# Softmax attention and a Mish layer, gated together, on one core: some normalising products on GpSimd, a new order, and another ending

## The chip, the cores and the metric

One core of a Trainium2 chip runs the kernel. The metric is device time in microseconds (us). The engines are TensorE (PE; PEld for its weight loads), VectorE (DVE), ScalarE (ACT), GpSimd (POOL) and SyncE (SP), which issues nearly all the DMAs.

## The reference

Two branches over 2048 tokens of width 640 are mixed by a gate per token.

```python
x = A_x                                             # 1 x 2048 x 640, bf16
g = sigmoid((x * gate_w).sum(-1, keepdims=True))
# A: 32 heads of 20
q, k, v = split_heads(x @ wqkv)
p = softmax(einsum("bhqd,bhkd->bhqk", q, k) * 20 ** -0.5)
a = merge_heads(einsum("bhqk,bhkd->bhqd", p, v)) @ wo
# B: 640 -> 1536 -> 640
h = einsum("bsd,df->bsf", x, w1) + b1
b = einsum("bsf,fd->bsd", h * tanh(softplus(h)), w2)
return g * a + (1 - g) * b
```

Both branches read the one x; an input B_x is taken and not used.

## The kernel before, in words

Queries are cut into 4 chunks of 512, heads into 8 groups of 4; a (chunk, group) pair is a group of work, and the last pair is cut into two of 256 queries. Each has 16 key tiles times 4 heads = 64 units, tiles of 128 keys x 512 queries. Three units make a step: 683 steps in all. For each step PE writes three score tiles into three PSUM banks (L1204), and ACT takes the exponential of all three in one instruction of 1536 columns (L1226, a wide step), or of two, 1024 columns (a narrow step). In a narrow step DVE evicts the third tile as an integer (L1271), and makes the exponential of it in pieces for up to four tiles at a time: fraction (L1335), product (L1339), power (L1343), all from SBUF to SBUF. Two sets of three banks alternate, so the scores of a step wait until ACT and DVE have read the step two before. PE multiplies the exponentials by V (L1463); a column of ones beside V sums them.

When a group ends, DVE copies the sums from PSUM to OUNG (L1552). SP turns the row of sums for the reciprocal (L1570), DVE inverts it (L1574), SP sends it to DRAM and back as a broadcast into BCT (L1575, L1581), and DVE multiplies OUNG by BCT (L1513): the normalising product, 128x512 in fp32 to bf16, into OTN for chunks 0 and 1 and into the free part of QT for chunks 2 and 3.

All else is fitted into gaps: projections, B's two matrix products, the Mish pieces on DVE, the output projection (L1048) and its mixture with B by the gate (L1054).

No loop of the chip's runs over this. The Python code is a planner: it lays out one straight list for each engine, by costs written in the file, and `pl.now` holds the time that it reckons each engine to be at. `work(until)` fills DVE's gaps from queues (`norm` for the normalising steps, `soon` for the pieces of the exponentials, `blend` for Mish, `bg`), `choose(s)` says whether step s is narrow, by DVE's lag and what is queued, and a table `NUDGE` shifts that choice for every eight steps. `Plan.run` gives the list out.

The last chunk's output projection is made in two parts: six groups early, into PART (fp32, in W2R's place), and the last two groups at the end. For the tokens of the second cut four tasks remain after the last exponential: two token tiles of 128 by two halves of 320 columns. One of them goes through ACT and POOL (L1902, L1904), three through DVE (L1054). Each half is stored by itself; SP issues six of these stores, ACT two (both L1080). Then each engine compares a flag and branches past a second program (for inputs whose exponents are too large), and SP waits for the stores:

```python
fast.run(eng, handle)
with handle.If(flags[eng] != 0):
    fast.wait_all(handle)
    full.run(eng, handle)
    ...
if eng == "sp":
    for op in outs:
        handle.wait_ge(fast.sems[op.key], op.count)
```

The line numbers that the prediction names are those of the kernel before. In the program after, the same steps have others: L1226 is L1287, L1271 is L1332, L1513 is L1576, L1054 is L1102, L1080 is L1131, L1993 is L2065.

Of the kernel before, what the change touches and what calls it, by code (L numbers as in the profile page):

```python
# [17 lines left out]
P = 128  # L18
# [5 lines left out]
NG = 8  # L24
# [13 lines left out]
OLD = 3  # L38
# [21 lines left out]
QUICK = 0.335  # L60
FAST = 0.335
# [8 lines left out]
RISK = {"pe": 0.1, "act": 0.3, "dve": 0.5, "pool": 1.2, "sp": 0.6}  # L70
CHAIN = 2.6
FILL = 2.5
GIVE_BACK = 40
# [9 lines left out]
SLOW_LOAD = 5.0  # L83
# [15 lines left out]
SPARE = 7  # L99
# [36 lines left out]
LEAD = 5  # L136
NUDGE = [0, 0, 0, 0, 0, 0, 0, 0, 0, 0, 0, 0, 0, 0, 0, 0, 0, 0, 0, 0, 0, 0, 0, 0, 0, 0, 0, 0, 0, 0, 0, 0, 0, 0, 0, 0, 0, 0, 0, 0, 0, 0, 0, 0, 0, 0, 0, 0, 0, 0, 0, 0, 0, 0, 0, -1, 0, 2, 0, 0, 0, 0, 0, 0, 0, 0.5, 3, 0, 0, 0, 3, 0, 1, 0.5, 0, 0, 0, 0, 0.5, 1, -0.5, 0, 0, -0.5, 0, 1]
# [12 lines left out]
class Plan:  # L150
# [3 lines left out]
    def __init__(self, prefix):  # L154
        self.prefix = prefix
        self.ops = []
        self.now = {e: 0.0 for e in ENGINES}
        self.kind = None
        self.passes = deque()
        self.queue = 0.0  # L160

    def add(self, eng, fn, deps=(), slot=None, cost=0.1, kind="F", tail=None, bulk=0.0):
        op = Op(eng, fn, [d for d in deps if d is not None], slot)
        at = self.now[eng]
        if eng == "pe":
            if kind != self.kind:
                at += SWITCH
                self.kind = kind
        for d in op.deps:
            if d.eng != eng or d.slot:  # L170
                at = max(at, d.t1 + HOP)
            elif eng == "dve":
                at = max(at, d.t1)
        self.now[eng] = at + cost
        if eng == "pe":
            self.passes.append((at + cost, cost))
        op.t1 = at + cost + (tail or (TAIL["sp"] if slot else TAIL[eng]))
# [42 lines left out]
    def run(self, eng, handle):  # L220
        for op in self.ops:
            if op.eng != eng:
                continue
# [25 lines left out]
def bass_gated_mix__softmax_full_mha__dense_activation_mish__prompt_kernel(  # L249
# [142 lines left out]
    def attention(pl, fast):  # L392
# [57 lines left out]
        def dve(fn, deps=(), cost=0.1, kind="F"):  # L450

            ready = max([pl.now["dve"], *(d.t1 + HOP for d in deps if d is not None)])
            work(ready + (LATER if fast and now["rate"] < BUSY and now["bank"] else SLACK))
            return pl.add("dve", fn, deps, cost=cost, kind=kind)
# [5 lines left out]
        def work(until):  # L460
            while True:
                best = None
                lined = sorted([lane for lane in (*soon, blend) if lane], key=lambda lane: lane[0][3])
                for rank, todo in enumerate((norm, *lined, bg)):
                    if todo:
                        cost, fn, dep = todo[0][:3]
                        op = dep() if dep else None
                        if op is False:
                            continue
                        begin = pl.now["dve"]  # L470
                        if op:
                            begin = max(begin, op.t1 if op.eng == "dve" and not op.slot else safe(op))
                        halve = len(todo[0]) > 4 and begin + cost > until
# [53 lines left out]
        if fast:  # L527
# [63 lines left out]
            q_blank = [pl.add("pool", lambda e, g=g: e.memset(QT[:, g, :], 0.0), cost=1.1) for g in range(1, NG)]  # L591
# [50 lines left out]
            def fetch(k, g, c, names):  # L642
# [14 lines left out]
                for dst, src in pairs:  # L657
                    op = pl.add("sp", lambda e, dst=dst, src=src: e.dma_start(dst, src), deps, slot, cost=0.5, bulk=1.3 if k else 0.1)
# [319 lines left out]
            def mish(ev, hb, hc, k):  # L978
# [9 lines left out]
                def piece(cost, fn, after=None):  # L988
                    def run():
                        last[0] = pl.add("dve", fn, [last[0]], cost=cost)  # L990
                        if after:
                            after(last[0])
                    blend.append((cost, run, lambda: last[0], due))
# [17 lines left out]
                piece(QUICK, scalar(B, W, MISH_IN))  # L1011
                piece(WIDE, times(B, W, B))
                piece(QUICK, scalar(B, B, MISH_MID))
                piece(WIDE, times(B, B, B))
                piece(QUICK, scalar(B, B, MISH_BY, MISH_BY * MISH_OUT))
# [55 lines left out]
        part_done = {}  # L1071

# [5 lines left out]
        def give(t, half, ev):  # L1078
            tb = (NC - 1) * 4 + t
            outs.append(pl.add(("sp", "act")[half and t in last_t], lambda e: e.dma_start(  # L1080
                out_ap[tb * P:(tb + 1) * P, of(half)], ended(t, half)), [ev], f"end{t}{half}", cost=0.6))

        def p_task(c, t, half, due, rest=False):
# [13 lines left out]
            def finish(bank, last):  # L1097
# [4 lines left out]
                add = PART[:, t, half, :] if rest else ball(tb)[:, of(half)]  # L1102
                if rest:
# [176 lines left out]
        def dve_by(fn, deps, cost, slack):  # L1280
# [3 lines left out]
            return pl.add("dve", fn, deps, cost=cost)  # L1284

        def close(batch):
# [15 lines left out]
            def piece(cost, fns, deps, after=None, split=False):  # L1302

                def run(some, each, mark):
                    def go():
                        for sp in some:
                            op = pl.add("dve", fns(sp), deps(), cost=each)
# [57 lines left out]
        def choose(s):  # L1365

            late = max(0.0, pl.now["dve"] - pl.now["act"]) - NUDGE[s // 8]
            urgent, other = (sum(t[0] for todo in some for t in todo) for some in ((norm, *soon), (blend, bg)))
# [5 lines left out]
            def tight(group, need):  # L1374
                ends = max((i for i, v in enumerate(near) if v[:2] == group), default=0)
                left = ends / TAKEN * EXP
                before = sum(t[0] for t in blend if t[3] < pl.now["act"] + left)
# [122 lines left out]
        def group_done(c, g, step, last):  # L1500
# [11 lines left out]
            def times(src, deps):  # L1512
                oung_free[0] = bc_read[0] = otn_done[(c, g)] = pl.add("dve", lambda e: e.tensor_tensor(  # L1513
                    otn(c, g, fast), src, BC, ALU.mult), [*deps, *reads()], cost=WIDE)
                if g == NG - 1:
                    otn_read[c % 2] = []
# [62 lines left out]
            def spread():  # L1579
# [5 lines left out]
                norm.append((WIDE, lambda: times(src, wide), lambda: wide[-1]))  # L1585
# [159 lines left out]
        def room():  # L1745
# [4 lines left out]
            owing = sum(t.dve for t in tasks) + sum(t[0] for todo in (norm, *soon, blend, bg) for t in todo)  # L1750
# [3 lines left out]
        def backlog():  # L1754

            return max(0.0, pl.now["dve"] - pl.now["act"]) + sum(t[0] for todo in (norm, *soon, blend, bg) for t in todo)
# [139 lines left out]
        for n, (bank, t, half) in enumerate(jobs):  # L1896
# [11 lines left out]
        for (t, half), op in sorted(ends.items(), key=lambda x: x[1].t1):  # L1908
            give(t, half, op)
# [79 lines left out]
    with nc.Block() as blk:  # L1989
        def program(eng):  # L1990
            def body(handle):
                fast.run(eng, handle)
                with handle.If(flags[eng] != 0):  # L1993
                    fast.wait_all(handle)
# [3 lines left out]
                if eng == "sp":  # L1998
                    for op in outs:
                        handle.wait_ge(fast.sems[op.key], op.count)  # L2000
# [36 lines left out]
```

## Time and profile before

| | |
|---|---|
| time, median of 3 runs | 789.43 us (788.85 to 789.61) |
| the profiled execution | 789.46 us, its span 787.6 us |
| granted TensorE clock | 0.998 |
| busy: PE, DVE, ACT, POOL | 721.0, 754.4, 771.0, 20.3 us |
| first exponential begins, last ends | 9.39 us, 778.5 us |

A row of the groups gives line, engine and operation, then output tile<-input tiles and their shapes, the count, then busy us in all and mean ns of one, then idle time of the engine just before, with what ended it. A row of the waits gives who waited for whom, us in total, times, and the longest. A row of the timeline gives start and length in us. A row for one line of the code gives the duration in ns (least, median, most) and the first and last start in us; "q" behind an engine is its sequencer or its DMA queue.

### The profile page before, as it was taken

To read this page: it belongs to the slowest core of one execution; us is meant where nothing else is said; L and a number is where in the kernel's file an instruction comes from. 1 tells how busy PE (TensorE), PEld (TensorE's weight loads), DVE (VectorE), ACT (ScalarE), POOL (GpSimd) and SP (SyncE) were. 2 spreads that over 40 slices of the span, in tenths; PEclk is the share of its full clock that TensorE was granted. 3 is DMA by queue.
4 is the path that set the end of the run, shared out by engine and by line. 5 is a ranking of instruction groups with operands and counts; after the bars stand their busy time and mean duration, and the time that the engine had idled before them with its cause. 6 is when DMAs were issued, how large, how long until landed. Compare 5 with 4: busy or idle time off the path is not lost.

```text
span 787.6 us, 16572 instructions
## 1 busy us (share of the span) xinstructions
PE 721.0 (92%) x6711; PEld 264.4 (34%) x6711; DVE 754.4 (96%) x1358; ACT 771.0 (98%) x715; POOL 20.3 (3%) x21
## 2 busy tenths in 40 slices
PE   8999999989899988999999999899989999989996
PEld 4333333233223333233333333333333333333332
DVE  4899999999999999999999999999999999999996
ACT  6999999999999999999999999999999999999995
POOL 8100000000000000000000000000000000000000
PEclk9999999999999999999999999999999999999999
DMA  8221310311233212402131201301121212101101
GB/s 188 75 60 53 100 54 15 94 59 53 66 104 84 65 51 73 129 15 52 52 80 51 69 22 51 85 16 45 47 85 50 82 44 56 32 23 28 25 20 39
DMA packets 77800, 47.13 MB, mean 60 GB/s; under 512 B 23916, under 2 KB 73700, under 8 KB 77668
## 3 DMA queue, kind: packets, MB, share of 16 engines
q1 hardware_dynamic: 77316, 45.80, 21.3%
q8 instruction: 56, 0.92, 0.5%
q14 instruction: 28, 0.23, 0.1%
q10 hardware_dynamic: 288, 0.16, 0.1%
q0 software_dynamic: 112, 0.01, 0.1%
HBM read 36.26 MB, written 7.52 MB: 56 GB/s over the span
## 4 chain that ended last, share of the span: by engine, by line
ACT 93%; PE 3%; DVE 3%; issue 0%; ACTq 0%
ACT ETS L1226 91%; ACT REG L983 2%; ACT W2R L983 1%; PE PS L1204 1%; PE PS L1463 1%; PE PS L562 0%; DVE HB L1054 0%; PE PS L1048 0%; PE PS L745 0%; PE PS L758 0%; PE PS L606 0%; DVE W2R L1054 0%; PE PS L950 0%; DVE QT L1271 0%; DVE QT L1513 0%
## 5 line engine op out<-in xcount | busy, mean ns | idle before, releaser
L1226 ACT ACTIVATE ETS<-PS 128x1024 bf16<-128x1024 f32 (+1 forms) x683 | 751.3, 1362 | 3.0 <-PE PS L1204 2.8
L1204 PE MATMUL PS<-QT,KT 32*128 32x512 bf16 (+1 forms) x2132 | 269.8, 378 | 53.0 <-ACT ETS L1226 42.7
L1463 PE MATMUL PS<-ETS,V_all 128*21 128x512 bf16 (+1 forms) x1690 | 166.5, 375 | 0.5 <-DVE OUNG L1552 0.5
L1204 PEld LDWEIGHTS PS<-QT,KT 32*128 32x128 bf16 x2132 | 67.5, 91 | 274.9 <-ACT ETS L1226 245.3
L1024 PE MATMUL PS<-W2R,HB 128*128 128x320 bf16 x384 | 69.0, 302 | 0.1
L1271 DVE TENSOR_SCALAR PADS<-PS 128x512 int16<-128x512 f32 x89 | 60.5, 683 | 6.8 <-PE PS L1204 6.5
L1271 DVE TENSOR_SCALAR QT<-PS 128x512 int16<-128x512 f32 x94 | 64.0, 683 | 2.2 <-PE PS L1204 1.6
L1271 DVE TENSOR_SCALAR OTN<-PS 128x512 int16<-128x512 f32 x89 | 60.4, 681 | 0.7 <-PE PS L1204 0.4
L950 PE MATMUL PS<-XB,REG 128*128 128x256 bf16 x360 | 55.1, 275 | 2.1 <-DVE XB L1031 0.9
L1463 PEld LDWEIGHTS PS<-ETS,V_all 128*21 128x21 bf16 x1690 | 42.5, 90 | 42.3 <-issue 26.3
L1008 DVE TENSOR_TENSOR U<-U 128x1024 f16<-128x1024 f16 x72 | 48.8, 677 | 0.1
L1024 PEld LDWEIGHTS PS<-W2R,HB 128*128 128x128 bf16 x384 | 30.9, 97 | 33.7 <-issue 19.7
L950 PEld LDWEIGHTS PS<-XB,REG 128*128 128x128 bf16 x360 | 29.0, 97 | 29.3 <-issue 27.0
L1271 DVE TENSOR_SCALAR REG<-PS 128x512 int16<-128x512 f32 x49 | 33.3, 683 | 0.7 <-PE PS L1204 0.5
L960 DVE TENSOR_TENSOR HB<-PS,B1T 128x512 bf16<-128x512 f32 x48 | 32.7, 682 | 0.8 <-PE PS L950 0.4
L1005 DVE TENSOR_SCALAR U<-U 128x1024 f16<-128x1024 f16 x72 | 30.0, 417 | 0.3
L1271 DVE TENSOR_SCALAR KT<-PS 128x512 int16<-128x512 f32 x40 | 27.3, 683 | 0.3
L1775 PE MATMUL PS<-KT 128*128 128x512 bf16 x88 | 25.1, 383 | 0.0
L1048 PE MATMUL PS<-WOQ,QT 128*128 128x320 bf16 x128 | 23.8, 302 | 0.8 <-DVE W2R L1054 0.3
L1048 PE MATMUL PS<-WOQ,OTN 128*128 128x320 bf16 x128 | 23.8, 302 | 0.2 <-issue 0.2
L667 PE MATMUL PS<-XB,REG 128*128 128x512 bf16 x80 | 23.2, 383 | 0.2 <-DVE WOQ L676 0.2
L1463 PE MATMUL PS<-QT,V_all 128*21 128x512 f16 x197 | 22.8, 384 | 0.4 <-DVE OUNG L1552 0.4
(188 smaller groups left out, 827.8 us busy)
## 6 DMA issues: line engine op xcount, KB each, us to landing
REG<-in_B_w_dram SPq DMA_DIRECT2D x36, 320.0 KB, 3.2
BCT<-SUMS SPq DMA_DIRECT2D x124, 64.0 KB, 2.1
W2R<-in_B_w_dram SPq DMA_DIRECT2D x12, 320.0 KB, 3.3
KT<-KS SPq DMA_DIRECT2D x28, 128.0 KB
QT<-QS SPq DMA_DIRECT2D x112, 20.0 KB
QS<-WOQ SPq DMA_DIRECT2D x16, 128.0 KB, 1.8
KS<-OTN SPq DMA_DIRECT2D x16, 128.0 KB, 1.7
W2R<-in_B_w_dram SPq DMA_DIRECT2D x1, 1920.0 KB, 8.3
```

What stands on the lines that cost most here:

```text
L950: return lambda e, bank: e.matmul(PS[:, bank, i * HW:(i + 1) * HW], w1b(n1)[:, f, i * P:(i + 1) * P], xt(c)[:, f, cols], start=(f == 0), s ...
L960: ev = dve(lambda e: e.tensor_tensor(hb, PS[:, bank, :].rearrange("p (i t) -> p i t", i=2), bias, ALU.add), [last, b_load, *guarded, *b_re ...
L983: ex = pl.add("act", lambda e: e.activation(U, h, AF.Tanh, scale=0.5, bias=-MISH_AT), [ev, u_free[0]], cost=0.95)
L1005: return lambda e: e.tensor_scalar(dst, src, *ops)
L1008: return lambda e: e.tensor_tensor(dst, one, two, ALU.mult)
L1024: return lambda e, bank: e.matmul(PS[:, bank, 0:HALF], HB[:, hc % 2, f, t * P:(t + 1) * P], W2[:, f, half * HALF:(half + 1) * HALF], start ...
L1048: return lambda e, bank: e.matmul(PS[:, bank, 0:HALF], otn(c, g, fast)[:, t * P:(t + 1) * P], WOG[:, g, half * HALF:(half + 1) * HALF], st ...
L1204: op = pl.add("pe", lambda e, i=i, g=real(g), tile=tile, j=j, cols=cols, c=c, of_q=of_q: e.matmul(scores(s)[:, i, cols], KT[32 * j:32 * j ...
L1226: e_op[s] = pl.add("act", lambda e: e.activation(ETS[:, s % NETS, 0:n, :], scores(s)[:, 0:n, :], AF.Exp, scale=SCALE, bias=LIFT if fast el ...
L1271: ev = dve_by(lambda e: e.tensor_scalar(block(batch["y"], n, I16), scores(s)[:, 2, :], SCALE * ULPS, BIAS, ALU.mult, ALU.add), [s_op[s], * ...
L1463: lasts[n] = pl.add("pe", lambda e, v=v, j=j, src=src[:, cols], of_q=of_q, count=count: e.matmul(PS[32 * j:32 * j + EW, ACC, of_q], v, src ...
L1775: pl.add("pe", lambda e: e.matmul(PS[:, bank, :], k[:, 0:P], k, start=True, stop=True), [free], cost=PASS, kind="S")
```

## The change

Four things change.

A normalising product may go to POOL. Each job in the queue `norm` that multiplies carries a second form. After every instruction that the planner puts on DVE from PSUM, `settle()` looks whether POOL could have begun the product behind the last DVE instruction that works on SBUF alone (kind "L") and ended it, by the planned 1.3 us, before the next. If so, the product goes to POOL, and is made to wait for that DVE instruction. `patient` lets DVE leave a product for up to `AWAIT` = 3 us before it takes it itself, except in the last 60 steps. The Mish pieces carry the second form only for a waiting time over 0, and `AWAIT_1` is 0.

The planner's constants and the table `NUDGE` are others, so that the whole order is laid out anew.

The last four tasks' mixtures are made on DVE alone, two of 640 columns, each over two PSUM banks, and each token tile is stored whole. ACT issues no store.

SP's list is cut in two at the first of these last stores. SP runs the head, compares the flag and branches past the second program, and then runs the stores and their waits under a second comparison. The other engines compare and branch where they did, at their lists' ends.

```diff
+ASIDE = 1.3
+APART = 0.1
+AWAIT = 3
+AWAIT_1 = 0
-LEAD = 5
-NUDGE = [0, 0, 0, 0, 0, 0, 0, 0, ...
+FETCH = (2.3, 3.0)
+LEAD = 10
+NUDGE = [0, -1.5, 0, 0.7, 0, 0.7, -3, 0.7, ...
...
+    def run(self, eng, handle, part=None):
+
+        mine = [op for op in self.ops if op.eng == eng]
+        if part:
+            at = next((n for n, op in enumerate(mine) if eng == "sp" and op.key[:3] == "end"), len(mine))
+            mine = mine[:at] if part == "head" else mine[at:]
+        for op in mine:
...
+        def settle():
+
+            while fast:
+                for todo in (blend, norm):
+                    job = todo[0][5] if todo and len(todo[0]) > 5 else None
+                    ready = job and job[0]()
+                    if not ready:
+                        continue
+                    line = pl.line
+                    i = len(line)
+                    while i and not line[i - 1][2]:
+                        i -= 1
+                    begin = max(ready.t1 + HOP, pl.now["pool"], line[i - 1][0])
+                    while i < len(line) and line[i][0] <= begin:
+                        i += 1
+                    if begin + job[1] + APART <= pl.now["dve"]:
+                        todo.popleft()
+                        job[2](line[i - 1][1])
+                        break
+                else:
+                    return
+
+        def patient(op, wait):
+
+            return now["step"] < NSLOT - CALM_END and pl.now["dve"] < op.t1 + wait
...
-                norm.append((WIDE, lambda: times(src, wide), lambda: wide[-1]))
+                norm.append((WIDE, lambda: times(src, wide), lambda: False if fast and patient(wide[-1], AWAIT) else wide[-1],
+                             0, None, (lambda: wide[-1], ASIDE, lambda dep: times(src, [*wide, dep], "pool"))))
...
+        for bank, t, _ in jobs[::2] if fast else ():
+            to = HB[:, t // 2, :, :].rearrange("p f t -> p (f t)")[:, t % 2 * D:(t % 2 + 1) * D].rearrange("p (a b) -> p a b", a=2)
+            ends[(t, 0)] = ends[(t, 1)] = pl.add("dve", lambda e, bank=bank, t=t, to=to: e.scalar_tensor_tensor(
+                to, PS[:, bank:bank + 2, 0:HALF], GATE[:, c * 4 + t:c * 4 + t + 1], PART[:, t, :, :], ALU.mult, ALU.add),
+                [lasts[bank], lasts[bank + 1], part_done[(t, 0)], part_done[(t, 1)], *gate_done], cost=0.75)
...
-                fast.run(eng, handle)
+                fast.run(eng, handle, "head")
                 with handle.If(flags[eng] != 0):
+                    fast.run(eng, handle, "stores")
                     fast.wait_all(handle)
                     full.run(eng, handle)
                     if eng == "sp":
                         full.wait_all(handle)
                 if eng == "sp":
-                    for op in outs:
-                        handle.wait_ge(fast.sems[op.key], op.count)
+                    with handle.If(flags[eng] == 0):
+                        fast.run(eng, handle, "stores")
+                        for op in sorted(outs, key=lambda op: op.t1):
+                            handle.wait_ge(fast.sems[op.key], op.count)
```

POOL, from the last small copy of the start to its branch, before. OUTT and REG hold gate and weights there; PADS is ACT's part of a mixture.

```order
L594 DMA OUTT<-in_gate_w_dram 128x5x1
L596 DMA ZEROS<-OTN 8x640
L598 COPY REG<-OUTT 128x5
L1691 TENSOR_LOAD FLAG
L1691 ISA x2
L1904 TENSOR_TENSOR HB<-PADS,W2R 128x320
L1993 COMPARE_AND_BRANCH
```

The same stretch of POOL after.

```order
L640 DMA OUTT<-in_gate_w_dram 128x5x1
L642 DMA ZEROS<-OTN 8x640
L644 COPY REG<-OUTT 128x5
L1576 TENSOR_TENSOR OTN<-OUNG,BCT 128x512 x4
L1755 TENSOR_LOAD FLAG
L1755 ISA x2
L1576 TENSOR_TENSOR OTN<-OUNG,BCT 128x512 x8
L1576 TENSOR_TENSOR QT<-OUNG,BCT 128x512 x5
L2065 COMPARE_AND_BRANCH
```

Seventeen products came to POOL, twelve of chunks 0 and 1 and five of chunks 2 and 3, and its part of the last mixture went.

DVE's last rows ahead of its branch, from behind the first cut's normalising on, before. U is the work area for the sums, W2R holds PART, HB takes the results.

```order
L1335 TENSOR_SCALAR REG<-OTN 128x2048
L1513 TENSOR_TENSOR QT<-OUNG,BCT 128x512
L1054 SCALAR_TENSOR_TENSOR W2R<-PS,GATE,XB 128x320
L1339 TENSOR_TENSOR REG<-REG,OTN 128x2048
L1343 TENSOR_SCALAR OTN<-OTN 128x2048
L1054 SCALAR_TENSOR_TENSOR W2R<-PS,GATE,XB 128x320
L1054 SCALAR_TENSOR_TENSOR HB<-PS,GATE,W2R 128x320 x2
L1536 STREAM_TRANSPOSE U<-PS 128x256
L1537 RECIPROCAL U<-U 128x8
L1538 STREAM_TRANSPOSE U<-U 128x256
L1542 TENSOR_TENSOR QT<-PS,U 128x256
L1054 SCALAR_TENSOR_TENSOR HB<-PS,GATE,W2R 128x320 x5
```

The same rows of DVE after.

```order
L1102 SCALAR_TENSOR_TENSOR W2R<-PS,GATE,XB 128x320
L1398 TENSOR_SCALAR OTN<-REG 128x2048
L1402 TENSOR_TENSOR OTN<-OTN,REG 128x2048
L1102 SCALAR_TENSOR_TENSOR W2R<-PS,GATE,XB 128x320
L1406 TENSOR_SCALAR REG<-REG 128x2048
L1102 SCALAR_TENSOR_TENSOR HB<-PS,GATE,W2R 128x320 x3
L1599 STREAM_TRANSPOSE U<-PS 128x256
L1600 RECIPROCAL U<-U 128x8
L1601 STREAM_TRANSPOSE U<-U 128x256
L1605 TENSOR_TENSOR QT<-PS,U 128x256
L1102 SCALAR_TENSOR_TENSOR HB<-PS,GATE,W2R 128x320
L1964 SCALAR_TENSOR_TENSOR HB<-PS,GATE,W2R 128x640 x2
```

The product of the last whole group (L1513) is gone from DVE's end, one more mixture of 320 stands ahead of the last transpositions, and the list ends with one of 320 and two of 640.

SP at the end of its list, before: the last group's normalising DMAs, the last stores and the branch.

```order
L1060 DMA out_dram<-OUTT 128x320
L1570 DMA RR<-OUNG 128x1x16
L1575 DMA SUMS<-RR 128x16
L1581 DMA BCT<-SUMS 32x512 x4
L1080 DMA out_dram<-HB 128x320 x6
L1993 COMPARE_AND_BRANCH
```

SP after: the same, up to the branch.

```order
L1108 DMA out_dram<-OUTT 128x320
L1633 DMA RR<-OUNG 128x1x16
L1638 DMA SUMS<-RR 128x16
L1644 DMA BCT<-SUMS 32x512 x4
L2065 COMPARE_AND_BRANCH
```

And SP where that branch leads to, behind the second program.

```order
L1644 DMA BCT<-SUMS 32x512 x4
L1131 DMA out_dram<-HB 128x320 x8
L2065 UNCONDITIONAL_BRANCH
L2072 COMPARE_AND_BRANCH
L1131 DMA out_dram<-HB 128x320 x4
L1131 DMA out_dram<-HB 128x640 x2
L2072 UNCONDITIONAL_BRANCH
```

The branch past the second program moved ahead of the last stores; four stores of 320 and two of 640 follow it, all on SP.

More of the change, by code (lines that the diff above doesn't have):

```diff
@@ L37 @@
 NETS = 6
-OLD = 3
+OLD = 4
 WAITED = 3
@@ L60 @@
 QUICK = 0.335
+ASIDE = 1.3
+ASIDE_1 = 1.2
+APART = 0.1
+AWAIT = 3
+SHARE = 0.3
+AWAIT_1 = 0
+CALM_END = 60
 FAST = 0.335
@@ L1102, in finish @@
                 add = PART[:, t, half, :] if rest else ball(tb)[:, of(half)]
+                if rest and fast and now["step"] >= NSLOT:
+                    n = len(aside)
+                    tmp = (EM, ER)[n % 2][:, 0:HALF]
+                    got = pl.add("act", lambda e: e.activation(
+                        tmp, PS[:, bank, 0:HALF], AF.Identity, scale=GATE[:, tb:tb + 1]),
+                        [last, *aside[-2:][:n - 1], *gate_done], cost=0.5)
+                    aside.append(pl.add("pool", lambda e: e.tensor_tensor(
+                        ended(t, half), tmp, add, ALU.add), [got, part_done[(t, half)]], cost=0.9))
+                    give(t, half, aside[-1])
+                    return got
                 if rest:
```

81 lines of the change are left out of this document (47 added, 34 removed).

## The prediction

> **What bounds the kernel now.** I read the page's busy times and chain first, then the waits of ACT, PE and DVE, then the groups by shape, then the timeline of the last 10 us.
>
> ```profile
> span 787.6 us, 16572 instructions
> PE 721.0 (92%) x6711; PEld 264.4 (34%) x6711; DVE 754.4 (96%) x1358; ACT 771.0 (98%) x715; POOL 20.3 (3%) x21
> ACT 93%; PE 3%; DVE 3%; issue 0%; ACTq 0%
> ACT ETS L1226 <- PE PS L1204: 2.8, 5, 1.0
> PE PS L1204 <- ACT ETS L1226: 42.7, 99, 1.2
> DVE PADS L1271 <- PE PS L1204: 6.5, 11, 2.9
> 9.39:130.00 120.61, 111.98 (x1192) 44.36 (x1189) 107.79 (x186) 118.81 (x110) 13.06 (x10) 1.00 0.27 75
> 300.00:450.00 150.00, 142.43 (x1225) 47.87 (x1219) 147.80 (x269) 149.85 (x141) 0.00 (x0) 1.00 0.24 66
> 778.50:787.60 9.10, 2.65 (x22) 1.25 (x21) 4.27 (x10) 0.54 (x2) 0.86 (x1) 0.86 0.29 82
> ```
>
> DVE and ACT look alike by busy time (96% and 98%), and the waits tell them apart. ACT's exponentials are 93% of the chain. Their idle time is 2.8 us in all, and PE ends it. PE's score matmuls L1204 wait for ACT 42.7 us, since an exponential must free the banks first. DVE waits for those matmuls too (6.5 us in 11 waits). So ACT paces the steady part: in the stretches (after the colon: length, then PE, PEld, DVE, ACT and POOL busy) it is full, 149.85 of 150.00, save for 1.8 us missing before 130 us. DVE is a second queue with little room. The last 9.1 us hold no exponential at all.
>
> **Exponentials and evictions.** The kernel splits the 683 exponential steps between ACT and DVE. A narrow step (1024 columns) leaves its third tile to DVE.
>
> ```profile
> L1226 ACT ACTIVATE ETS<-PS 128x1024 bf16<-128x1024 f32 x407 | 443.2, 1191 | 0.8 <-PE PS L1204 0.8
> L1226 ACT ACTIVATE ETS<-PS 128x1536 bf16<-128x1536 f32 x276 | 439.0, 1615 | 2.2 <-PE PS L1204 2.0
> L1271 DVE TENSOR_SCALAR QT<-PS 128x512 int16<-128x512 f32 x94 | 64.0, 683 | 2.2 <-PE PS L1204 1.6
> L1513 DVE TENSOR_TENSOR OTN<-OUNG,BCT 128x512 bf16<-128x512 f32 x16 | 10.9, 680 | 0.0
> L1335 DVE TENSOR_SCALAR OTN<-OTN 128x2048 int16<-128x2048 int16 x11 | 7.5, 679 | 0.0
> L1339 DVE TENSOR_TENSOR OTN<-OTN 128x2048 f16<-128x2048 f16 x8 | 9.7, 1216 | 0.0
> L1343 DVE TENSOR_SCALAR PADS<-PADS 128x2048 int16<-128x2048 int16 x20 | 13.7, 682 | 0.0
> L1904 POOL TENSOR_TENSOR HB<-PADS,W2R 128x320 bf16<-128x320 f32 x1 | 0.9, 862 | 755.8 <-ACT PADS L1902 755.8
> ```
>
> Counted in the order of the changed program, narrow steps go from 407 to 411 and wide ones from 276 to 272, since 17 of the 31 normalising products have left DVE. A wide one lasts 1615 ns and a narrow one 1191, so each step changed saves ACT 0.424 us: 4 x 0.424 = 1.7 us off the pacing engine. This is the part that I trust most, since ACT is full.
>
> DVE's own sum: 17 of the products (L1513, 0.680 us) go to POOL, -11.6 us. Four more evictions (0.683) add 2.7 us. Their later steps, by the three rows for four tiles (0.679 + 1.216 + 0.682 = 2.58 us per four tiles), add 2.6 us. Net -6.3 us of DVE time. I put that at nothing on the end: no row has ACT waiting for DVE, and the time that DVE gains turns into longer waits for PE. If ACT's waits do come from DVE by way of PE, the gain is at most the 1.8 us of idle time before 130 us.
>
> The product on POOL is new in the steady part. The nearest row is POOL's 862 ns for 320 columns of fp32 with two inputs; 512 columns make 0.862 x 512 / 320 = 1.38 us (estimate). From below it can't beat the 0.86 us of the smaller one; from above I take twice the estimate, 2.8 us. I take 1.38. Nobody waits for it soon: its readers are the output projections, and the next group refills OUNG about 769 / 33 = 23 us later (exponentials run from 9.4 to 778.5 us over 33 groups). In the changed program each product waits for its last broadcast DMA and for one DVE instruction, behind which DVE nearly always has two to four evictions from PSUM (0.683 us each), 2.0 us for three. The product is over before DVE's next instruction on SBUF alone.
>
> The Trainium skill (SBUF — State Buffer, Who interferes with whom) speaks against such an arrangement: a DVE instruction with two SBUF inputs, or in a two-port mode, and a GpSimd instruction that reads SBUF exclude each other for their whole length. By it the sum stays as it is while products keep inside the evictions, and rival 2 begins where they don't; before, POOL's only product ran beside PSUM readers alone, so no row here shows a collision.
>
> **The order set anew.** The table and constants change which PE task fills which gap. The first 18 ACT instructions are the same in both orders. What ACT loses in waits is then drawn again:
>
> ```profile
> 28.89 1.45 ACT L1226 ACTIVATE ETS<-PS 128x1536 bf16<-128x1536 f32 x1 [0.25 <-PE PS L1204]
> 31.10 1.45 ACT L1226 ACTIVATE ETS<-PS 128x1536 bf16<-128x1536 f32 x1 [0.75 <-PE PS L1204]
> ```
>
> Bounds: -1.8 us if the early idle time goes, +2 us if as much comes again. I take 0, as nothing in the trace favours a side.
>
> **The tail.**
>
> ```profile
> 777.19 1.33 ACT L1226 ACTIVATE ETS<-PS 128x1024 bf16<-128x1024 f32 x1
> 780.01 1.48 PE L1048 MATMUL PS<-WOQ,QT 128*128 128x320 bf16 x8
> 780.30 0.42 DVE L1542 TENSOR_TENSOR QT<-PS,U 128x256 bf16<-128x256 f32 x1
> 780.64 2.37 DVE L1054 SCALAR_TENSOR_TENSOR HB<-PS,GATE,W2R 128x320 bf16<-128x320 f32 x5
> 777.86 6.31 SPq L1080 DMA_DIRECT2D out_dram<-HB  x6
> 782.13 1.53 ACTq L1080 DMA_DIRECT2D out_dram<-HB  x2
> out_dram<-OUTT SPq DMA_DIRECT2D x24, 80.0 KB, 1.6
> QS<-WOQ SPq DMA_DIRECT2D x16, 128.0 KB, 1.8
> L1054 DVE SCALAR_TENSOR_TENSOR HB<-PS,GATE,W2R 128x320 bf16<-128x320 f32 x7 | 3.5, 544 | 1.4 <-PE PS L1048 1.4
> L832 DVE CAST V_all<-PS 128x480 bf16<-128x480 f32 x15 | 9.7, 648 | 0.0
> L803 DVE CAST V_all<-PS 128x320 bf16<-128x320 f32 x8 | 3.9, 486 | 1.6 <-PE PS L795 1.5
> L1993 SPq COMPARE_BRANCH  x1: 53/53/53, 784.2 to 784.2; - x1
> L2000 SPq EVENT_SEMAPHORE  x5: 17/28/28, 786.9 to 787.2; - x5
> L1989 DVEq DRAIN  x1: 40/40/40, 785.1 to 785.1; - x1
> L1989 ACTq DRAIN  x1: 80/80/80, 786.4 to 786.4; - x1
> L1993 ACTq COMPARE_BRANCH  x1: 54/54/54, 783.7 to 783.7; - x1
> L1989 SPq DRAIN  x1: 13/13/13, 787.4 to 787.4; - x1
> ```
>
> Before, DVE's last mixture ends at 780.64 + 2.37 = 783.0, SP's last store has been issued at 777.86 + 6.31 = 784.2, and SP branches then. Its first wait behind the branch comes at 786.9, that is 2.7 us later. A store of 80 KB lands 1.6 us from its issue, and SP's last issue begins before 784.2: all the data is there by 785.8 at the latest. SP's branch, not the data, sets the end, with 0.7 us from first wait to the end of the span. ACT is the runner-up: it branches behind its two stores at 783.7, and drains at 786.4.
>
> After, SP branches behind the last broadcast of the sums, while DVE still computes, and its 2.7 us lie beside the last exponentials. What is left to wait for:
>
> - DVE's five mixtures of 320 are 0.457 us apart, (2.37 - 0.544) / 4 with 0.544 for the last one's length. Now one of 320 stands there and then two of 640. By the two CAST rows 160 columns cost 162 ns, so 320 more cost 0.324: a 640 takes 0.868, and two start 0.78 apart. The first starts when its two matmuls are done. PE's eight end at 780.01 + 1.48 = 781.49, one each 0.185 us, so the second of the last four ends near 781.1, which is also when DVE is free (780.64 + 0.457). From 781.2, 0.78 + 0.868 more make 782.85, say 782.9, against 783.0: nothing gained by itself. ACT's and POOL's share of a mixture is gone, and it lay beside DVE's.
> - SP issues the last store at 782.9, no longer behind two queues' issues. It carries 160 KB; from 1.6 us at 80 KB and 1.8 at 128 KB I take 1.9, and it lands at 784.8.
> - The closing 0.7 us stays: 785.5. DVE's drain at 785.1 (its branch isn't moved) and SP's drain 0.2 us ahead of the end set 785.3 as a floor. ACT's drain falls to soon after its last exponential, as it issues no store.
>
> So the tail ends at 785.5 where it ended at 787.6: -2.1 us. Bounds: -2.3 from DVE's drain; 0 if SP still pays the 2.7 us at the end (rival 1). If the cover for SP's branch were gone, it would cost those 2.7 us.
>
> The Trainium skill (Runtime: NRT & Kernel Launch, Instruction fetch mechanics) says that a taken branch out of the fetched window waits for a DMA of its target. By that rule DVE keeps its gap and SP's second, nearby jump costs nothing; the 2.7 us on SP agree with it, and the sum would be the same.
>
> **The sum.** The profiled execution took 789.46 us with a span of 787.6, next to the median of 789.43. 789.46 - 1.7 (four steps) + 0 (waits) - 2.1 (tail) = 785.7 us, 0.5% less. Own range: waits from -1.8 to +2 and the tail from -2.3 to -1.9 give 783.7 to 787.9. About 0.2%, 1.6 us, is what a measurement of this kernel can tell from no change.
>
> **Rivals.**
>
> 1. The move of SP's branch doesn't do what it says: another jump, at the end of SP's new block, or another engine's drain, takes its place at the end. For it: DVE's drain already stands at 785.1. Against it: SP's jump at the end of its waits took no more than 0.2 us before (last wait 787.2, drain 787.4). Time: 785.7 + 2.1 = 787.8, at the edge of no change. Chance 0.10.
> 2. POOL holds DVE back. If a product takes 2.8 us instead of 1.38, it reaches 0.7 us past three evictions, and DVE's next step on SBUF waits, with the evictions behind it, and so PE's scores and ACT. 17 x 0.7 = 12 us on DVE; I let half reach ACT, as DVE has some waits of its own to lose: 785.7 + 6 = 791.7, slower. It decides from a product of about 2.0 us on. Against it: 862 ns in the only row, and 1.38 by its columns. The skill's rule above names the same collision. Chance 0.07.
> 3. The new order makes PE late. Three narrow steps in a row stand 51 times in the new order and 30 times in the old one; a narrow step gives PE 0.42 us less to write the next scores among its other tasks. If each of the 21 more brings one wait like the smallest visible, 0.25 us, ACT loses 5.3 us: 791.0, slower. Against it: 2.8 us of such waits in five places over all 683 steps, with 30 such runs among them. Chance 0.15.
>
> **How the numbers follow.** The forecast holds 0.68, nearly all of it faster; rival 1 lies half on either side of the 0.2% bound; rivals 2 and 3 are slower, with a little of rival 3's milder cases in between. That makes faster 0.74, same 0.07, slower 0.19. The range is the forecast's own widened to 783.4 for the estimates in the tail, and upward to 789.0, which takes in rival 1 and the mild part of rival 3; the rest of rivals 2 and 3 is left out.
>
> **What would show it.** Right: 411 narrow and 272 wide steps at the same lengths; ACT still full from 130 us on; POOL with 17 products of about 1.4 us; DVE some 6 us less busy with longer waits for PE; SP's branch before 778 us; the span ending about 7.0 us behind the last exponential, not 9.1. Wrong: ACT waits for L1204's successor well over 3 us, DVE steps on SBUF longer than their 680 ns beside POOL's products, or a gap of over 2 us between the last store's landing and the end.

## The result and the profile after

After: **784.12 us**, median of 3 runs (784.11 to 784.28). Before: 789.43. The ratio is 0.9934 [0.992, 0.9948], that is 5.3 us less; the prediction was 785.7, 3.7 us less. Two further sets of five runs of the same kernel, beside the experiments, gave 784.72 and 784.41.

The page of the kernel after: span, busy times, shares of the chain.

```profile
span 782.3 us, 16554 instructions
PE 717.5 (92%) x6701; PEld 261.4 (33%) x6701; DVE 749.0 (96%) x1325; ACT 768.6 (98%) x714; POOL 40.9 (5%) x37
ACT 93%; DVE 3%; PE 2%; DMA 0%; issue 0%; SPq 0%
```

The stretches that were shown of before, and the last 5.5 us (length, then busy time of PE, PEld, DVE, ACT and POOL, each with its count; TensorE clock; DMA share; GB/s):

```profile
9.34:130.00 120.66, 113.74 (x1206) 45.09 (x1204) 109.07 (x196) 119.83 (x112) 16.88 (x13) 1.00 0.28 76
300.00:450.00 150.00, 141.60 (x1224) 46.55 (x1225) 146.39 (x251) 150.00 (x142) 3.80 (x3) 1.00 0.22 60
776.80:782.30 5.50, 1.33 (x9) 0.51 (x7) 2.98 (x5) 0.00 (x0) 0.00 (x0) 1.00 0.31 100
```

ACT still paces: full between 300 and 450 us, and before 130 us it now misses 0.8 us where it missed 1.8. DVE's busy time fell by 5.4 us, POOL's doubled. The groups, by shape, of ACT's exponentials and of POOL's product:

```profile
L1287 ACT ACTIVATE ETS<-PS 128x1024 bf16<-128x1024 f32 x411 | 444.4, 1210 | 0.5 <-PE PS L1265 0.5
L1287 ACT ACTIVATE ETS<-PS 128x1536 bf16<-128x1536 f32 x272 | 430.1, 1629 | 1.3 <-PE PS L1265 1.3
L1576 POOL TENSOR_TENSOR OTN<-OUNG,BCT 128x512 bf16<-128x512 f32 x12 | 15.2, 1270 | 362.9 <-DVE PADS L1402 113.0 <-DVE QT L1406 45.8 <-DVE KT L1398 44.5
```

And the exponentials' row of ACT's waits (us in all, times, longest):

```profile
ACT ETS L1287 <- PE PS L1265: 1.9, 3, 1.0
```

The counts are the forecast ones. Waits of the exponentials went from 2.8 us in five places to 1.9 in three. Twelve of POOL's 17 products stand in this row, at 1.27 us each.

The ending of the kernel after, from the timeline (start, length):

```profile
777.26 0.42 DVE L1605 TENSOR_TENSOR QT<-PS,U 128x256 bf16<-128x256 f32 x1
777.60 0.54 DVE L1102 SCALAR_TENSOR_TENSOR HB<-PS,GATE,W2R 128x320 bf16<-128x320 f32 x1
778.22 1.68 DVE L1964 SCALAR_TENSOR_TENSOR HB<-PS,GATE,W2R 128x640 bf16<-128x640 f32 x2
773.72 6.59 SPq L1131 DMA_DIRECT2D out_dram<-HB  x6
```

And by line (duration in ns: least, median, most; first and last start): SP's branch, its second comparison and its waits for the stores, then the drains of ACT, DVE and SP (an instruction near the end of each engine's list):

```profile
L2065 SPq COMPARE_BRANCH  x1: 58/58/58, 762.0 to 762.0; - x1
L2072 SPq COMPARE_BRANCH  x2: 38/39/40, 764.6 to 781.9; - x2
L2075 SPq EVENT_SEMAPHORE  x4: 17/28/28, 780.4 to 781.9; - x4
L2061 ACTq DRAIN  x1: 80/80/80, 776.7 to 776.7; - x1
L2061 DVEq DRAIN  x1: 41/41/41, 781.4 to 781.4; - x1
L2061 SPq DRAIN  x1: 13/13/13, 782.1 to 782.1; - x1
```

SP branches at 762.0 and is at the next comparison at 764.6: the 2.6 us are still paid, 11 us ahead of the last exponential's end. The last store is issued at 779.92, its wait has passed by 781.9, and SP's drain follows.

**Where the 5.3 us are**, profiled execution against profiled execution. The last exponential ends at 775.49 us and ended at 778.51: 3.0 us. Summed from the start of each exponential to the start of the next, 1.7 of them are the four steps. What lies over the shortest distance of each kind of step (one set of distances for all kernels; called gaps below) went from 10.99 to 9.66 us, 1.3 less. From the last exponential to the end of the span, here called the ending, it is 6.8 us and was 9.1: 2.3 us.

How far to trust such sums: the three profiles of the kernel after agree from the first to the last exponential to 0.01 us (764.76 us each), the five of kernels in the old order to 0.3 (767.50 to 767.80). The ending is looser: 6.8, 7.1 and 6.7 us for the kernel after.

### The profile page after: what moved, and what is told of

It reads as the page before. It is cut to its first block, busy times and chain, and to the rows that moved or that the text cites. A ratio compares the mean times of both kernels' runs of the same rounds, so it can differ in the third digit from the quotient of the medians.

```text
span 782.3 us, 16554 instructions
## 1 busy us (share of the span) xinstructions
PE 717.5 (92%) x6701; PEld 261.4 (33%) x6701; DVE 749.0 (96%) x1325; ACT 768.6 (98%) x714; POOL 40.9 (5%) x37
## 4 chain that ended last, share of the span: by engine, by line
ACT 93%; DVE 3%; PE 2%; DMA 0%; issue 0%; SPq 0%
ACT ETS L1287 91%; ACT REG L1029 2%; ACT W2R L1029 1%; PE PS L1265 1%; DMA OTN<-in_A_x_dram 0%; PE PS L1526 0%; PE PS L652 0%; DVE REG L1332 0%; DVE W2R L1102 0%; DVE OTN L1402 0%; PE PS L804 0%; DVE QT L1605 0%; PE PS L996 0%; PE PS L1096 0%; DVE W2R L1332 0%
## 5 line engine op out<-in xcount | busy, mean ns | idle before, releaser
L1526 PE MATMUL PS<-ETS,V_all 128*21 128x512 bf16 (+1 forms) x1687 | 164.1, 375 | 0.0
L1332 DVE TENSOR_SCALAR OTN<-PS 128x512 int16<-128x512 f32 x105 | 71.0, 681 | 1.7 <-PE PS L1265 1.4
L1332 DVE TENSOR_SCALAR QT<-PS 128x512 int16<-128x512 f32 x91 | 62.0, 682 | 1.7 <-PE PS L1265 1.2
L1056 DVE TENSOR_TENSOR U<-U 128x1024 f16<-128x1024 f16 x72 | 48.8, 678 | 0.0
L1332 DVE TENSOR_SCALAR KT<-PS 128x512 int16<-128x512 f32 x51 | 34.8, 683 | 2.4 <-PE PS L1265 2.1
L1576 POOL TENSOR_TENSOR OTN<-OUNG,BCT 128x512 bf16<-128x512 f32 x12 | 15.2, 1270 | 362.9 <-DVE PADS L1402 113.0
L1576 POOL TENSOR_TENSOR QT<-OUNG,BCT 128x512 bf16<-128x512 f32 x5 | 6.4, 1273 | 357.5 <-DVE OTN L1398 154.1
```

What stands on the lines that cost most here:

```text
L1056: return lambda e: e.tensor_tensor(dst, one, two, ALU.mult)
L1332: ev = dve_by(lambda e: e.tensor_scalar(block(batch["y"], n, I16), scores(s)[:, 2, :], SCALE * ULPS, BIAS, ALU.mult, ALU.add), [s_op[s], * ...
L1526: lasts[n] = pl.add("pe", lambda e, v=v, j=j, src=src[:, cols], of_q=of_q, count=count: e.matmul(PS[32 * j:32 * j + EW, ACC, of_q], v, src ...
```

## The experiments

The questions, in this order: is the ending's gain SP's branch? Is DVE's relief worth nothing, as the prediction had it? What would POOL cost if its products were longer, or more? What is the new order worth by itself? Each kernel is compared with the kernel before on the same chip.

### The ending in parts

Four kernels, all with the order of before up to the last exponential. **a_branch**: SP's list cut and branch ahead, and all eight stores of 80 KB on SP:

```diff
-            outs.append(pl.add(("sp", "act")[half and t in last_t], lambda e: e.dma_start(
+            outs.append(pl.add("sp", lambda e: e.dma_start(
...
-                fast.run(eng, handle)
+                fast.run(eng, handle, "head")
...
+                    with handle.If(flags[eng] == 0):
+                        fast.run(eng, handle, "stores")
```

> The kernel before with one thing changed: SP branches ahead of the last chunk's stores and issues all eight 80 KB stores itself; mixtures as before (one by way of ACT and POOL, the rest 320 wide). Theory: SP's branch set the end (2.7 us from it to the first wait), so the end moves to the last store's landing: last issue near 783.4, landed near 785.0, end near 785.6, 2.0 us less, about 787.4. Rival (another engine's branch takes its place): ACT's drain at 786.4 came behind ACT's stores, so if ACT's branch after its last activation still ends late, under 1 us is gained, about 788.6 or more.

**b_wide**: only the two mixtures of 640 and the whole stores, all on SP, with the branch behind them as before.

> The kernel before with the other half of the ending: the last four mixtures as two of 640 on DVE and whole stores, all on SP, but SP's branch stays behind the last store. Theory: DVE ends at 782.9 as before, the last store is issued 0.8 us sooner, and the 2.7 us of the branch and the closing 0.7 follow: 0.8 us less, about 788.6. Rival (the width and the single store are where the tail's gain comes from): 2 us less, about 787.4.

**c_tail**: both together.

> The kernel before with the whole new ending and nothing else; the steady part's order is the old one, instruction for instruction. Theory: the tail from the last exponential's end to the span's end falls from 9.1 to 6.8 us as in the kernel after: 2.3 us less, about 787.1, and the other 3.0 us of the change lie in the steady part. Rival (the steady part moved the tail too): well under 2 us less.

**a2_act**: as a_branch, without its first pair of diff lines: ACT keeps its two stores.

> The kernel before with SyncE's branch ahead of the stores and nothing else: ScalarE keeps its two stores, the mixtures stay 320 wide. With all eight stores on SyncE the last store landed 2.9 us after its issue and the span stayed at 787.4. Theory A: the late issues of eight stores in one queue made the landing late. Then the last store lands 1.6 to 1.9 us after its issue, ScalarE's drain behind its own late branch (786.4 before) becomes the last one, and the span ends at 786.6 to 786.9. Theory B: code loads of the other engines' branches stand in the way of whatever is stored after about 6 us behind the last exponential. Then the last store lands 2.5 to 3 us after its issue again, and the span ends at 787.2 or later.

| kernel | time us | ratio to before | SP branches | last store on SP, issue begins | its wait passed | ACT's drain | end of span behind last exponential |
|---|---|---|---|---|---|---|---|
| before | 789.4 | 1 | 784.2 | 783.72 | 787.2 | 786.4 | 9.1 |
| b_wide | 789.25 | 0.9998 [0.9989, 1.0007] | 783.6 | 783.02 | 786.7 | 779.0 | 8.9 |
| a_branch | 790.26 | 1.0011 [1.0002, 1.002] | 765.9 | 784.04 | 787.0 | 784.3 | 9.2 |
| a2_act | 788.49 | 0.9992 [0.9983, 1.0001] | 766.0 | 782.96 | 785.5 | 785.9 | 7.9 |
| c_tail | 787.86 | 0.9984 [0.9975, 0.9993] | 765.9 | 782.91 | 784.7 | 778.9 | 7.0 |
| after | 784.12 | 0.9934 [0.992, 0.9948] | 762.0 | 779.92 | 781.9 | 776.7 | 6.8 |

The columns behind the ratio are read from one profiled execution each, in us from the start of its span. Those of a_branch (789.22 us) and c_tail (786.98) are the fastest of their eleven, so the views show these two at their best; what the other executions of a_branch lose beside it is not in the trace. Below stand two views of each of three kernels: the timeline's row of SP's stores (it ends when the last one has been issued), and by line SP's waits for them and ACT's drain. a_branch:

```profile
777.52 6.96 SPq L1083 DMA_DIRECT2D out_dram<-HB  x8
```

```profile
L2006 SPq EVENT_SEMAPHORE  x5: 17/28/28, 784.5 to 786.9; - x5
L1992 ACTq DRAIN  x1: 80/80/80, 784.3 to 784.3; - x1
```

a2_act:

```profile
777.67 5.99 SPq L1083 DMA_DIRECT2D out_dram<-HB  x6
```

```profile
L2006 SPq EVENT_SEMAPHORE  x5: 17/28/28, 784.4 to 785.5; - x5
L1992 ACTq DRAIN  x1: 81/81/81, 785.9 to 785.9; - x1
```

c_tail:

```profile
777.52 5.73 SPq L1085 DMA_DIRECT2D out_dram<-HB  x6
```

```profile
L2016 SPq EVENT_SEMAPHORE  x4: 17/28/28, 783.5 to 784.7; - x4
L2002 ACTq DRAIN  x1: 81/81/81, 778.9 to 778.9; - x1
```

In all three, SP's branch is out of the way, and what is left is when the last store begins, how fast it lands (landing is the moment that the profile shows it done), and ACT's drain. With eight stores on one queue the last is issued 1.1 us later than in a2_act (784.04 against 782.96; one of the issues took 1.13 us) and lands 0.4 us more slowly (2.9 against 2.5 us from its issue): these two put the last landing back by 1.4 us. With ACT's two stores kept, the data is there at 785.5, but ACT's drain at 785.9, behind its own late branch, comes after it. Only wide stores, few and on SP alone, with the branch ahead, leave an ending of 7.0 us. So the mixtures alone gain nothing (b_wide); the branch alone loses 0.8 us by the medians with all stores on SP (a_branch), or gains about 1 us with an interval that takes in none (a2_act); and both together gain 1.6 us by the medians, 2.5 by the profiled spans, of which 2.1 are the ending. Of my two theories for a2_act, A had the order of events right (ACT's drain is last), but the landing of 2.5 us lay in B's range, and the profiled span of 786.2 us below both forecasts. Where the 0.4 us of slower landing in a_branch come from is left open. Theory B's loads of program code are a rival that no run sets apart: from 780 to 788 us the DMA view counts seven packets of kind "instruction" in a_branch and in a2_act and four in c_tail, where ACT has branched long before.

### DVE's relief at an unchanged order

**d_on_dve** is the kernel after with the 17 products put back on DVE; PE, ACT and SP run the same lists, and the planner's clock is left as if POOL did them.

```diff
...
+                    was = pl.now["dve"], list(pl.line)
+                    op = pl.add("dve", lambda e: e.tensor_tensor(
+                        otn(c, g, fast), src, BC, ALU.mult), given, cost=0.0, kind="F")
+                    pl.now["dve"], pl.line = was
+                    pl.now["pool"] = at + ASIDE
```

> The kernel after with its order kept on PE, ACT and SP, but with the 17 products put on DVE, each at the place in DVE's list from which it was sent to POOL. DVE gets 17 x 0.68 = 11.6 us more. Theory (DVE time is worth nothing by itself, ACT paces): 784.1 to 785. Rival (DVE is a second bound, and its lag reaches ACT by way of PE's scores): a good part of the 11.6 us shows, 788 or more.

786.41 us (785.7 to 787.88), ratio 0.9962 [0.9949, 0.9976]: 1.7 to 2.3 us slower than the three sets of the kernel after (784.12 to 784.72), 1.45 faster than c_tail. The sum from start to start is 766.57 us, against 764.76 in each of the three profiles of the kernel after. The theory that the relief is worth nothing falls. The chain on its page:

```profile
ACT 86%; DVE 8%; PE 4%; issue 1%; DMA 1%; SPq 0%
```

PE's longest waits for DVE in it:

```profile
PE PS L1265 <- DVE PADS L1332: 1.9, 4, 0.8
PE PS L1265 <- DVE KT L1332: 1.4, 4, 0.8
PE PS L1265 <- DVE OTN L1332: 1.2, 3, 0.6
```

Of these rows the kernel after has one, and smaller; its chain had DVE at 3%:

```profile
PE PS L1265 <- DVE OTN L1332: 0.6, 1, 0.6
```

DVE holds back ACT, by way of PE: its late evictions keep score banks from PE, and the next scores are late. ACT's start-to-start sum has 11.47 us over the shortest distances, against 9.66: 1.8 us, in many pieces of 0.1 to 0.4 us that the waits of ACT hardly list (1.9 us in three places in the kernel after, 2.2 in five in d_on_dve). The traces show why: a narrow exponential lasts 1.2 us, but the next one starts 0.90 us after it where nothing holds it, so a delay of up to some 0.3 us leaves no idle time to list. The pieces lie all over the kernel: 0.4 us before 130 us, 0.7 from there to 300, 0.1 to 450, 0.4 to 600, 0.2 behind. The ending took 0.3 us more, no more than it differs between profiles of the kernel after. All this is the worth of the relief at this order; what a plan made for DVE alone would lose is not shown.

### Longer products on POOL: rival 2's price

**e_twice**: each of the 17 products twice over on POOL, all else in the same order.

```diff
+                if eng == "pool":
+                    deps = [*deps, *reads()]
+                    at = pl.now["pool"]
+                    first = pl.add("pool", lambda e: e.tensor_tensor(otn(c, g, fast), src, BC, ALU.mult), deps, cost=0.0)
+                    deps = [*deps, first]
+                    pl.now["pool"] = at
```

> The changed kernel with each of the 17 GpSimd products done twice over (2.55 us instead of 1.27, the second write over the first); every other engine has the same instructions in the same order. The price that rival 2 named: a product then reaches 0.5 to 0.7 us past three evictions. If GpSimd and a VectorE instruction with two SBUF inputs shut each other out, and VectorE's lost time reaches ScalarE as it did when the products were put back on VectorE (2.3 us for 17 x 0.68 = 11.6 us), the 17 products take up to 17 x 0.7 = 12 us from VectorE and the kernel gets 1 to 2.5 us slower: 785.1 to 786.6. If VectorE is not held by a running product, nothing changes: 784.1. Rival 2 as it was priced (half of the 12 us reaches the end) gives 790.

788.51 us (788.16 to 790.52), ratio 0.9991 [0.9982, 1.0]: 3.8 us more than the kernel after beside it (784.72). Sixteen DVE instructions were longer than their like, by some 11 us together. One of them from the timeline, with POOL's second product beside it:

```profile
407.42 1.27 POOL L1582 TENSOR_TENSOR OTN<-OUNG,BCT 128x512 bf16<-128x512 f32 x1
407.05 0.68 DVE L1332 TENSOR_SCALAR QT<-PS 128x512 int16<-128x512 f32 x1
407.64 1.59 DVE L1056 TENSOR_TENSOR U<-U 128x1024 f16<-128x1024 f16 x1
409.16 0.68 DVE L1402 TENSOR_TENSOR PADS<-PADS,QT 128x1024 f16<-128x1024 f16 x1
```

And the chain on the page:

```profile
ACT 73%; DVE 18%; PE 8%; issue 1%
```

The eviction at 407.05 reads PSUM and keeps its 0.68 us beside the product. L1056, which reads only SBUF (0.68 us elsewhere), is dispatched at 407.64 and ends at 409.23, 0.54 us behind the end of POOL's product. Rival 2's mechanism is real, and its 12 us on DVE were some 11; a third of it reached the end, not half. So the time lies between the 786.6 of the one theory and the 790 of the other.

### More products on POOL

**h_all_pool** puts all 31 there, each behind the DVE instruction ahead of its old place:

```diff
...
+                    op = pl.add("pool", lambda e: e.tensor_tensor(
+                        otn(c, g, fast), src, BC, ALU.mult), [*given, pl.line[-1][1]], cost=0.0, kind="L")
```

> The changed kernel with the other 14 products taken from VectorE to GpSimd too (31 of 31), each released by the VectorE instruction ahead of its old place; all other instructions in the same order. 0 on GpSimd gave 786.4, 17 gave 784.1. If the relief of VectorE is worth the same by the product (2.3 / 17 = 0.135 us), 14 more bring 1.9 us: 782.2. If only products beside PSUM evictions pay, because GpSimd holds back VectorE instructions with two SBUF inputs, the 14 (whose places the planner found unfit) cost up to 0.6 us each on VectorE as much as they spare: 784.1 and above. If VectorE's time no longer matters after the first 17, nothing changes either, but then no VectorE instruction is longer beside a product.

786.08 us (784.78 to 786.62), ratio 0.9954 [0.9941, 0.9968], 1.4 us more than the kernel after beside it; the ranges of the two overlap, but the sum from start to start is 0.9 us longer in the trace. Of the 14 new places eight met a DVE instruction on SBUF alone, and nine such instructions (one beside the 17th product, as in the kernel after) were some 4.5 us too long. This is the second case of the expectation. Here both sides lost, a product (0.31 us over its 1.27) and the DVE instruction (0.68 in its like):

```profile
578.75 0.68 DVE L1057 TENSOR_TENSOR U<-U 128x1024 f16<-128x1024 f16 x1
578.98 1.58 POOL L1586 TENSOR_TENSOR QT<-OUNG,BCT 128x512 bf16<-128x512 f32 x1 [27.59 <-DVE OTN L1333]
579.35 1.76 DVE L1399 TENSOR_SCALAR OTN<-OTN 128x2048 int16<-128x2048 int16 x1
```

**i_five_more** leaves only the five of the 14 that held up no DVE instruction, 22 in all. It was meant as a version faster than both kernels.

```diff
...
+                nth[0] += eng == "dve"
+                if eng == "pool" or not fast or nth[0] not in (2, 6, 9, 11, 13):
```

> The changed kernel with 22 products on GpSimd: to the 17 come those five of the other 14 that no VectorE instruction was longer beside, and that VectorE did not wait for, when all 31 stood there. Everything else in the same order. If an unhindered product is worth 0.135 us, as the first 17 were, five bring 0.7 us: 783.6 beside 784.3 of the changed kernel. If the five places were already slack, no difference.

784.77 us (784.31 to 784.89), beside 784.41 (783.92 to 784.51) of the kernel after itself: no gain, and in the trace 0.4 us more between the exponentials. Three of the five products took 1.58 us there, as they did in h_all_pool. The two sets of the kernel after, as **z_after** beside e_twice, h_all_pool and f_no_pool (784.72 us, 784.0 to 786.27, ratio 0.9942 [0.9929, 0.9956]), and as **z2_after** beside i_five_more, a2_act and old_table (784.41 us, ratio 0.9936 [0.9922, 0.9949]), were there as the yardstick:

> The changed kernel itself, as it is, beside the three others on one chip: 784.1 us, 0.993 of the kernel before.

> The changed kernel as it is, once more, beside the next run: 784.1 to 784.7 us.

The worth of DVE's relief is not by the product: the first 17 brought some 2 us, the next five nothing. That PE by then waits for DVE in only a few places fits this, but no run shows it to be the reason.

### The order and its table

**f_no_pool**: the kernel after, where no product may go to POOL, laid out anew (`if False and begin + ...` in `settle`).

> The changed kernel's planner and table with no product offered to GpSimd: the plan is laid anew, with 398 narrow and 285 wide exponentials instead of 411 and 272, since VectorE has no room for more evictions. If the count of narrow steps carries the gain, 13 x 0.424 = 5.5 us are lost: 789.6. If instead VectorE's load sets small waits of ScalarE, as with the products put back at an unchanged order, some 2 us of waits come on top or go away with the lighter VectorE (13 evictions fewer): between 788 and 791. If the count didn't matter, 786.4 as with the products on VectorE at 411.

801.88 us (801.4 to 803.52), ratio 1.0159 [1.0145, 1.0173], well above what any of my cases gave. ACT's waits:

```profile
ACT ETS L1287 <- PE PS L1526: 7.2, 7, 2.1
ACT ETS L1287 <- PE PS L1265: 3.2, 6, 1.0
ACT PADS L1157 <- PE PS L1096: 3.1, 1, 3.1
```

By the trace: 13 narrow steps fewer are 5.5 us, waits and small gaps between the exponentials 10.7 us more, and the ending 1.9 us more. Products stay on DVE here, but `patient` still lets them wait up to 3 us for a place on POOL that never comes, so it isn't a fair "without POOL"; d_on_dve is.

**old_table**: the kernel after with the table `NUDGE` of before.

> The changed kernel with the table NUDGE of the kernel before: products are still offered to GpSimd, but the plan comes out with 400 narrow and 283 wide exponentials (411 and 272), and 9 products on GpSimd. If the count of narrow steps carries all, 11 x 0.424 = 4.7 us are lost: 788.8 to 789.4. If a table that does not fit the rest also costs waits, as it did without GpSimd (some 10 us of waits on top of the narrow steps), it is 795 to 800.

795.19 us (794.78 to 795.96), ratio 1.0075 [1.0061, 1.0089], 10.8 us more than the kernel after beside it. Eleven narrow steps fewer are 4.7 us, gaps between the exponentials 4.1 us more (13.71 against 9.65), and the ending 2.2 us more, with two mixtures on ACT and POOL again; the plan also sends 9 products to POOL, not 17. That is the second case: the narrow steps are less than half of what the table does.

## Why the prediction was right, and where not

**The narrow steps, -1.7.** Right: 411 and 272, and d_on_dve, which has the new order and ending but not the relief, stands 1.45 us below c_tail, which has the ending alone.

**DVE's relief, put at nothing.** The step that failed. "No row has ACT waiting for DVE" was true of the rows and not of the engines: PE waits for DVE between the two, and ACT's pieces of 0.1 to 0.4 us mostly stay below what the waits list. The bound given for that path, at most 1.8 us, was right in size, and that is luck: it stood for the idle time before 130 us, and only 0.4 us of the relief lie there. The relief measured 1.7 to 2.3 us by the medians, 1.8 between the exponentials in the trace, and comes from all over the kernel. Less the 0.5 us that the order costs, and with 0.2 from the tail, it makes up 1.5 of the 1.6 us by which the forecast was too high.

**The new order, 0 between -1.8 and +2.** By itself it costs 0.5 us of gaps (11.47 in d_on_dve against 10.99 before, with four evictions more on DVE), so 0 was near. In d_on_dve the gaps before 130 us are 0.7 us less than in the kernel before, and those behind 1.2 more. The bounds were narrow for what an order can do: two other ones, old_table and f_no_pool, cost 4 and 11 us in gaps alone.

**The tail, -2.1.** -2.3 in the trace of the kernel after; c_tail has -2.1 in its trace and -1.6 by the medians. The forecast's steps hold: branch ahead, last mixture 4.4 us behind the last exponential (forecast 4.4), landing 1.9 us after the issue, 0.5 us from there to the end where 0.7 were taken, DVE's drain 0.9 ahead of the end. But it gave the whole to the move of the branch, "nothing gained by itself" by the wide mixtures. a_branch, a2_act and b_wide show that neither half brings the gain without the other, so the size was right with half of its cause missing. One reading led there: "all the data is there by 785.8 at the latest" took the 1.6 us of the steady part for the ending, where the stores of the kernel before land 2.3 to 3.2 us from their issue when several come together. Its last one, issued at 783.72, lands at 786.0, only 0.9 us ahead of SP's first wait. The branch alone had no 2 us to give.

**POOL's product.** 1.27 us, where 1.38 was the estimate; 16 of the 17 held up no DVE instruction.

**Rival 1** (something else takes the branch's place) is what a_branch and a2_act are: the queue of stores, and ACT's drain. In the change itself both causes were taken away. **Rival 2** (POOL holds DVE back) has the right mechanism, and needs longer products or other places: at 1.27 us it happens once. In the kernel after, the 17th product and the DVE instruction beside it; then the same step in the kernel before, with POOL idle:

```profile
768.19 1.27 POOL L1576 TENSOR_TENSOR QT<-OUNG,BCT 128x512 bf16<-128x512 f32 x1 [62.08 <-DVE U L1599]
768.80 0.95 DVE L1605 TENSOR_TENSOR QT<-U 128x256 bf16<-128x256 f32 x1
772.25 0.42 DVE L1542 TENSOR_TENSOR QT<-U 128x256 bf16<-128x256 f32 x1
```

The Trainium skill (SBUF — State Buffer, Who interferes with whom) says that whichever issues first keeps the shared port pair for its whole instruction and the other blocks. The rows here, of e_twice and of h_all_pool agree, in both directions: L1056 ends 0.54 us behind POOL's product, and POOL's product of 1.58 us began while L1057 ran. **Rival 3** (PE late for triple-narrow runs) was not seen: waits of ACT for scores fell from 2.8 to 1.9 us, where 5.3 us more were priced.

## What to carry to other kernels

An engine that waits for nobody by name can still be paced by another through a third: before a relief is put at nothing, look at the waits of the engine in between, and sum start to start, not the listed waits. In these runs, work moved to GpSimd pays where its neighbours on VectorE read PSUM, and costs on both engines where they work on SBUF alone; and the second helping paid nothing. An ending is a race of several late things: take each away alone, and see what is next, before giving the gain to one.

## What was not expected of the hardware

SP's issue of an 80 KB store took 0.33 to 1.13 us when several came close together, and these stores landed mostly 2.5 to 3.1 us from their issue (1.8 to 3.3 in all), where 24 stores of the same size in the steady part took 1.6 at the median. The two stores of 160 KB took 1.8 to 2.3 us in c_tail and after. A branch past the second program cost SP 2.6 to 2.8 us early and 2.7 to 2.9 us late, so where it stands changes who waits for it and not its price.
